# Attention and a cosine feed-forward: six plain blocks instead of four ahead of Strassen pairs

## The chip, the cores and the metric

The kernel runs on one core of a Trainium2 chip. Five engines work at once, each through its own instructions in a fixed order: TensorE (PE, matmuls; PEld is its weight loads), VectorE (DVE), ScalarE (ACT), GpSimd (POOL) and SyncE (SP, which here only issues transfers). Matmuls write to PSUM (eight banks of 128 x 512 floats), everything else lives in SBUF, inputs and outputs in HBM, and DMA queues move data between them. The metric is the device time of one execution in microseconds (us).

## The reference

Eight batches, eight heads, 576 positions, head size 64. Heads 0 to 3 see the last 32 positions ("local"), heads 4 to 7 see earlier positions of the same residue modulo 32 ("strided"). The result, 4608 tokens by 512, goes through a feed-forward with 2048 hidden columns and the activation h * cos(h).

```python
scores = scale * np.matmul(q, k.transpose(0, 1, 3, 2))
mask_local = (rel >= 0) & (rel < stride)
mask_strided = (rel >= 0) & (pos[None, :] % stride == pos[:, None] % stride)
...
attn = np.exp(scores)
attn = attn / (np.sum(attn, axis=-1, keepdims=True) + 1e-09)
return np.matmul(attn, v).astype(np.float32)
...
h = x @ w_in
g = h * np.cos(h)
return (g @ w_out).astype(np.float32)
```

## The kernel before

**Numbers in two halves.** Each matmul operand of the feed-forward is kept as a rounded part and a remainder (`hi`, `lo`), and a product is three matmuls: hi*hi, hi*lo, lo*hi. A split is one cast (ACT or DVE) and one subtraction (POOL, sometimes DVE).

**Blocks.** The 4608 tokens are 12 blocks of 384 (TB). A *plain* block goes through 16 chunks, one for each 128 hidden columns. A chunk (`chunk`, L475) is `hidden` (12 matmuls into one PSUM bank, L436), the curve h*cos(h) on ACT and DVE (L442 to L449), its split, and, three chunks later (LAG), `outer`: 9 matmuls into three accumulators (L460). A *pair* is two blocks multiplied by Strassen's recursion in Winograd's form: for each *quad* (a pair of hidden chunks, 8 quads in all) seven products of 6 matmuls (L684) into the banks a and b stand for the 48 matmuls of four chunks; DVE and ACT add the products (p1, u2, u3, h), `curved` makes g, and the outer matmuls (L712), 12 tiles of three a quad, are used one quad later as *fillings* between the products (FILL). The weights of the pairs, sums and differences of blocks of `w_in`, are formed once by `combine` (L519) from the weights in SBUF, written to HBM (wis, wos), and loaded again quad by quad (`load_quad`, L669).

**Attention** is cut into units: four strided and three local ones a batch, 56 in all. A unit is a load of q and k and one of v, score matmuls (L291 local, L343 strided), a softmax on DVE, POOL and ACT, a transposition (PE through L360, or DVE's L300), and product matmuls (L312, L374) whose result is copied to `x_t` or `x_l` and written to xT in HBM by ACT's queue. Outside the first stage a unit spreads over several chunks: in a burst (`burst`, L504) the products of unit k-3 and the scores of unit k are interleaved when they use PE in the same tile shape.

**Stages.** (1) The 14 units of batches 0 and 1. (2) Blocks 0 and 1 side by side, while the weights are loaded and split. (3) Blocks 2 and 3 with batches 2 to 4 beside them: bursts stand ahead of chunks as KNOTS says, and `combine` is called every third chunk. (4) Four pairs, with batches 5 to 7 beside the first 21 quads: scores in bank a, transposition in b, products in a and b, between the products of the quad. Stages 3 and 4 use different pools; stage 4 begins with `stage_x` (L646), which loads 4 x 2 pieces of x, forms 3 further operands each, and `split_operand` (L661) for all seven. At each later pair's boundary the seven operands are replaced one by one while the last quad uses them.

Chunks of stage 3 are counted from block 2 below, so chunk 0 is its first. Each engine runs its own list in order; a scheduler that models times writes the lists, and may put an instruction earlier than the code calls it. `in_turn` (L183) keeps PE's matmuls from block 2 on in the order of the code.

Of the kernel before, what the change touches and what calls it, by code (L numbers as in the profile page):

```python
# [26 lines left out]
P = 128  # L27
# [36 lines left out]
KNOTS = ((3, 0), (19, 16), (30, 23))  # L64
# [3 lines left out]
PLAIN = 4  # L68
NPAIR = (NTB - PLAIN) // 2
NQ = NFC // 2  # L70
PB = 5
FILL = (2, 2, 2, 2, 2, 1, 1)

# [7 lines left out]
def attention_cos_ffn(ctx, tc, qkl, vl, qkvs, w_in, w_out, eye, eye16, mask_l0, mask_l, mask_s, out):  # L81
# [5 lines left out]
    plain = ExitStack()  # L87
    ps_h = plain.enter_context(tc.tile_pool(name="ps_h", bufs=2, space=bass.MemoryType.PSUM, reuse_waits="tile"))
    ps_o = plain.enter_context(tc.tile_pool(name="ps_o", bufs=1, space=bass.MemoryType.PSUM, reuse_waits="tile"))
# [32 lines left out]
    wp = plain.enter_context(tc.tile_pool(name="wp", bufs=1, reuse_waits="tile"))  # L122
    wi_h, wi_l, wo_h, wo_l = [], [], [], []
    for f in range(NFC):
        for held, name, shape in (
            (wi_h, "wi_h", [P, NKC, P]), (wi_l, "wi_l", [P, NKC, P]), (wo_h, "wo_h", [P, DM]), (wo_l, "wo_l", [P, DM]),
        ):
            held.append(wp.tile(shape, F32R, name=f"{name}{f}"))
    xs = plain.enter_context(tc.tile_pool(name="xs", bufs=2 * NKC, reuse_waits="tile"))
# [61 lines left out]
    class Attention:  # L191
# [6 lines left out]
        def __init__(self, stack, plain, scores, transposed, products, ld_bufs):  # L198

            self.plain, self.banks = plain, None  # L200
# [12 lines left out]
        def bank(self, kind):  # L213
            pool, name = self.banks.pop(0) if self.banks else next(kind)
            return pool.tile([P, 512], F32, name=name)

        def score_bank(self, mask):
# [10 lines left out]
            if self.banks:  # L228
                return self.bank(None)
# [48 lines left out]
        def local(self, b, u):  # L278
# [49 lines left out]
        def strided(self, b, p, u):  # L328
# [10 lines left out]
            rows = GP if self.banks else GB  # L339
            s_ps = self.score_bank(mask)  # L340

            def score(t, i):
                self.scored = self.pe(nc.tensor.matmul(  # L343
                    s_ps[half(1 - i, rows), t * GB:(t + 1) * GB], qk[half(i), t * GB:t * GB + rows], k_t[half(i), t],
                    start=not self.plain, stop=True, skip_group_check=True,
                ))
# [3 lines left out]
                if rows == GP or SU * u + t // 2 * 2 + i < NG  # L350
# [80 lines left out]

    def hidden(j, f, x_hi, x_lo):
        h = ps_h.tile([P, 512], F32, name="h")[:, :TB]
# [22 lines left out]
    def outer(j, f, g_hi, g_lo, acc):  # L456
        for t in range(NTT):
# [7 lines left out]
            if f == NFC - 1:  # L465
                o = op.tile([P, DM], F32, name="o")
                if t % 2:
                    nc.vector.tensor_copy(out=o, in_=acc[t])
                else:
                    nc.scalar.copy(out=o, in_=acc[t])  # L470
                nc.sync.dma_start(out=out[j * TB + t * P:j * TB + (t + 1) * P, :], in_=o)
# [47 lines left out]
    def combine(sp, q):  # L519

        wf = sp.tile([P, 2, DM], F32, name="wf", bufs=1)
        for n, f in enumerate((q, q + NQ)):
            nc.gpsimd.tensor_tensor(
                out=wf[:, n], in0=wi_h[f].bitcast(F32).rearrange("p c n -> p (c n)"),
                in1=wi_l[f].bitcast(F32).rearrange("p c n -> p (c n)"), op=ALU.add,
            )
# [10 lines left out]

        s1 = formed(4, a21, a22, ALU.add)
        s2 = formed(0, s1, a11, ALU.subtract)
        formed(3, a11, a21, ALU.subtract)  # L540
        formed(6, a12, s2, ALU.subtract)
        for i, f, k in ((1, q, 0), (2, q, 1), (5, q + NQ, 1)):
            for part, w in enumerate((wi_h, wi_l)):
# [3 lines left out]
                )  # L547
        for f in (q, q + NQ):
            for part, w in enumerate((wo_h, wo_l)):
                nc.sync.dma_start(out=wos[f][:, part], in_=w[f].bitcast(F32))  # L550

    first = [x_operands() for _ in range(2)]
    with ExitStack() as loading:
        cv = loading.enter_context(tc.tile_pool(name="cv", bufs=3, reuse_waits="tile"))
        with ExitStack() as stack:
# [3 lines left out]
                stack, True, ((ps_h, "h"), (ps_h, "h"), (ps, "acc0")), ((ps_o, "acc0"), (ps_o, "acc1")),  # L559
# [21 lines left out]
        rp = plain.enter_context(tc.tile_pool(name="rp", bufs=2, side="right", reuse_waits="tile"))  # L581
        gp = plain.enter_context(tc.tile_pool(name="gp", bufs=LAG + 1, side="right", reuse_waits="tile"))
# [18 lines left out]
    with ExitStack() as stack:  # L601
        op = stack.enter_context(tc.tile_pool(name="op", bufs=3, reuse_waits="tile"))
        sp = stack.enter_context(tc.tile_pool(name="sp", bufs=1, reuse_waits="tile"))
        ps = stack.enter_context(tc.tile_pool(name="ps", bufs=1, space=bass.MemoryType.PSUM, reuse_waits="tile"))
        att = Attention(stack, False, *(((ps, f"acc{i}"),) for i in range(3)), ld_bufs=2)
# [25 lines left out]
    plain.close()  # L631

    with ExitStack() as stack:
        rp, gp = (
            stack.enter_context(tc.tile_pool(name=name, bufs=bufs, side="right", reuse_waits="tile"))
            for name, bufs in (("rp2", 3), ("gp2", 6))
# [269 lines left out]
```

## Time and profile before

| | |
|---|---|
| median of 3 runs | 1028.52 us (1023.87 to 1029.41) |
| the profiled execution | 1028.36 us, of which the span of instructions is 1026.6 |
| stages 1 and 2 with the first three chunks of block 2 | to 201.75 us |
| stage 3, the rest | to 387.95 us |
| stage 4 | to the end |

The busy share of an engine is an average over stages. A wait is put down to the instruction that ended last before it. The granted clock is the share of full speed that PE was given in a stretch (1.00 is 2.4 GHz, half of it 1.2 GHz). Ends of matmuls are modelled, so counts in a window can miss or add a few at its edges.

### The profile page before, as it was taken

How to read it: one execution, taken by the hardware profiler on the slowest of the kernel's cores; microseconds unless marked ns; L12 is line 12 of the kernel's file. 1: busy time of each engine (PE TensorE's matmuls, PEld its weight loads, DVE VectorE, ACT ScalarE, POOL GpSimd, SP SyncE). 2: the span in 40 equal slices, each digit the busy share in tenths (PEclk: the TensorE clock that was granted, in tenths of full speed). 3: DMA queues.
4: the chain of work that ended last, by engine and by line, in shares of the span. 5: the costliest groups of instructions: out<-in, count | busy, mean ns of one | idle time of the engine just before them, and what ended most of it. 6: DMA issues, size and time to landing. Idle time of an engine off the chain costs nothing. (4 is left out here: it accounts for less than half of the span.)

```text
span 1026.6 us, 20627 instructions
## 1 busy us (share of the span) xinstructions
PE 933.2 (91%) x7852; PEld 806.1 (79%) x7852; DVE 584.6 (57%) x1085; ACT 533.2 (52%) x1095; POOL 438.9 (43%) x434
## 2 busy tenths in 40 slices
PE   8779999998689992999987999989989989999998
PEld 5568999977578882887876887867878778898997
DVE  5667654487776525554567444546763545754453
ACT  3557776465466532554535444535654434654543
POOL 3645655589864325332345222325532223532221
PEclk9899999999899996899989899999999989999999
DMA  9768764346554228866555665655585546575501
GB/s 299 261 192 280 247 225 134 108 144 220 185 171 135 72 65 327 318 201 189 198 177 183 207 195 174 203 196 167 183 269 178 176 122 185 169 262 173 167 21 61
DMA packets 97618, 190.98 MB, mean 186 GB/s; under 512 B 10992, under 2 KB 35056, under 8 KB 97520
## 3 DMA queue, kind: packets, MB, share of 16 engines
q1 hardware_dynamic: 89024, 181.57, 53.8%
q10 hardware_dynamic: 8496, 8.09, 2.4%
q8 instruction: 62, 1.02, 0.4%
q14 instruction: 36, 0.29, 0.1%
HBM read 149.26 MB, written 40.37 MB: 185 GB/s over the span
## 5 line engine op out<-in xcount | busy, mean ns | idle before, releaser
L712 PE MATMUL acc<-wo,g_hi 128*128 128x512 f32 x768 | 246.8, 404 | 0.0
L699 POOL TENSOR_TENSOR g_lo<-r,g_hi 128x384 fp32r<-128x384 f32 x128 | 133.4, 1043 | 232.6 <-ACT g_hi L698 120.8
L684 PE MATMUL a<-xo_hi,wq 128*128 128x384 f32 x512 | 158.3, 350 | 8.4 <-DVE t_sb L245 7.0
L712 PEld LDWEIGHTS acc<-wo,g_hi 128*128 128x128 f32 x768 | 146.5, 194 | 15.1
L684 PE MATMUL b<-xo_hi,wq 128*128 128x384 f32 x384 | 124.0, 364 | 35.8 <-DVE x_l L324 23.5
L712 PE MATMUL acc<-wo,g_lo 128*128 128x512 f32 x384 | 153.2, 399 | 0.0
L693 DVE SCALAR_TENSOR_TENSOR r<-r,h 128x384 f32<-128x384 int32 x128 | 81.2, 634 | 76.2 <-ACT r L692 75.1
L453 POOL TENSOR_TENSOR g_lo<-r,g_hi 128x384 fp32r<-128x384 f32 x64 | 70.1, 1095 | 107.3 <-issue 56.2
L684 PEld LDWEIGHTS a<-xo_hi,wq 128*128 128x128 f32 x512 | 98.1, 195 | 16.6 <-DVE t_sb L245 8.3
L684 PEld LDWEIGHTS b<-xo_hi,wq 128*128 128x128 f32 x384 | 75.0, 198 | 41.6 <-DVE x_l L324 24.5
L694 ACT ACTIVATE r<-r,biases 128x384 f32<-128x384 f32 x128 | 78.9, 617 | 52.6 <-DVE r L693 51.9
L695 DVE TENSOR_TENSOR r<-r,h 128x384 f32<-128x384 f32 x128 | 85.7, 670 | 29.0 <-ACT r L694 27.5
L698 ACT CAST g_hi<-r 128x384 fp32r<-128x384 f32 x128 | 65.5, 512 | 66.6 <-DVE r L695 66.1
L436 PE MATMUL h<-x_hi,wi_h 128*128 128x384 f32 x256 | 89.1, 348 | 3.2 <-DVE r L449 3.1
L692 ACT ACTIVATE r<-h 128x384 int32<-128x384 f32 x128 | 67.0, 523 | 44.5 <-DVE h L788 21.9
L684 PE MATMUL a<-xo_lo,wq 128*128 128x384 f32 x256 | 88.5, 346 | 0.0
L712 PEld LDWEIGHTS acc<-wo,g_lo 128*128 128x128 f32 x384 | 74.6, 194 | 17.5
L436 PE MATMUL h<-x_hi,wi_l 128*128 128x384 f32 x256 | 86.3, 337 | 0.0
L436 PE MATMUL h<-x_lo,wi_h 128*128 128x384 f32 x256 | 85.9, 336 | 0.0
L460 PE MATMUL acc<-wo_h,g_hi 128*128 128x512 f32 x192 | 77.7, 405 | 0.0
L460 PE MATMUL acc<-wo_l,g_hi 128*128 128x512 f32 x192 | 77.0, 401 | 0.0
L460 PE MATMUL acc<-wo_h,g_lo 128*128 128x512 f32 x192 | 74.6, 396 | 0.0
(136 smaller groups left out, 1733.4 us busy)
## 6 DMA issues: line engine op xcount, KB each, us to landing
wq<-wis SPq DMA_DIRECT2D x224, 256.0 KB, 2.8
wo<-wos SPq DMA_DIRECT2D x64, 512.0 KB, 4.2
qk<-in_qkvs SPq DMA_DIRECT2D x32, 324.0 KB, 3.4
qk<-in_qkl SPq DMA_DIRECT2D x24, 416.0 KB, 3.7
out<-o SPq DMA_DIRECT2D x36, 256.0 KB, 2.6
raw<-in_w_in SPq DMA_DIRECT2D x16, 512.0 KB, 5.4
raw<-in_w_out SPq DMA_DIRECT2D x16, 512.0 KB, 3.7
wis<-sr SPq DMA_DIRECT2D x32, 256.0 KB, 2.2
```

The source lines that it names most:

```text
L436: mm = nc.tensor.matmul(h, w[f][:, c], x[c], start=(i == 0), stop=(i == len(ops) - 1))
L453: nc.gpsimd.tensor_tensor(out=g_lo, in0=r, in1=g_hi.bitcast(F32), op=ALU.subtract)
L460: mm = nc.tensor.matmul(acc[t], g[:, ts], w[f], start=(f == 0 and i == 0), stop=(f == NFC - 1 and i == 2))
L684: in_turn(nc.tensor.matmul(bank, w[:, n, c], part[:, c], start=start and i == 0, stop=stop and i == len(ops) - 1, skip_group_check=True,))
L692: nc.scalar.activation(out=k, in_=h, func=AF.Copy, scale=1.0 / (2.0 * math.pi), bias=0.25)
L693: nc.vector.scalar_tensor_tensor(out=r, in0=k, scalar=-2.0 * math.pi, in1=h, op0=ALU.mult, op1=ALU.add)
L694: nc.scalar.activation(out=r, in_=r, func=AF.Sin, bias=quarter)
L695: nc.vector.tensor_tensor(out=r, in0=r, in1=h, op=ALU.mult)
L698: nc.scalar.copy(out=g_hi, in_=r)
L699: nc.gpsimd.tensor_tensor(out=g_lo, in0=r, in1=g_hi.bitcast(F32), op=ALU.subtract)
L712: in_turn(nc.tensor.matmul(acc, g[gn][:, ts], w[:, wn], start=done == 0 and i == 0, stop=done == NFC - 1 and i == 2,))
```

## The change

Six blocks are plain and three pairs remain. All 42 units of batches 2 to 7 stand beside the 61 chunks of stage 3 (KNOTS), none in the pairs; both copies of `x_l` are ACT's. `combine` is cut in four parts, called one a chunk from chunk 14 on. From chunk 49 on `staging` loads and splits the operands of the first pair, into the x tiles of block 4 and weight slots that block 5 has used. All weights lie in one pool of 64 slots; in the pairs the slots 20 to 37 take the products' weights, 38 to 51 those of the outers, and 0 to 19 and 52 to 63 hold two sets of x operands, so that the next pair's operands are made while this pair runs. The last three outers of block 5 are the first fillings of the pairs.

```diff
-KNOTS = ((3, 0), (19, 16), (30, 23))
+KNOTS = ((3, 0), (13, 9), (59, 44))
...
-PLAIN = 4
+PLAIN = 6
...
+X_AT, WQ_AT, WO_AT, Y_AT = 0, 20, 38, 52
+SUMS_AT = 14
+STAGED_AT = 49
...
-            if self.plain:
-                nc.scalar.copy(out=x_t[1], in_=a_ps[1][:, :LQ])
-            else:
-                nc.vector.tensor_copy(out=x_t[1], in_=a_ps[1][:, :LQ])
+            nc.scalar.copy(out=x_t[1], in_=a_ps[1][:, :LQ])
...
+    def staging(pool, c, k, pieces):
+
+        at = (PLAIN + 2 * c) * TB
+        b12, b11, b22, b21, t1, t2, t4 = (
+            pool.tile([P, TB], F32, name=name) for name in ("b12", "b11", "b22", "b21", "t1", "t2", "t4")
+        )
+        for raw, row, n in ((b12, 0, 1), (b11, 0, 0), (b22, 1, 1), (b21, 1, 0)):
+            nc.sync.dma_start(out=raw, in_=xT[:, 2 * row + k, at + n * TB:at + (n + 1) * TB])
+        yield
+        nc.vector.tensor_tensor(out=t1, in0=b12, in1=b11, op=ALU.subtract)
+        nc.vector.tensor_tensor(out=t2, in0=b22, in1=t1, op=ALU.subtract)
+        for i, raw in enumerate((t2, b11, b21, b12, t1, t4, b22)):
+            if i == 2:
+                nc.vector.tensor_tensor(out=b12, in0=b22, in1=b12, op=ALU.subtract)
+                nc.vector.tensor_tensor(out=t4, in0=b21, in1=t2, op=ALU.subtract)
+            hi, lo = (piece() for piece in pieces[i])
+            nc.scalar.copy(out=hi, in_=raw)
+            nc.gpsimd.tensor_tensor(out=lo, in0=raw, in1=hi.bitcast(F32), op=ALU.subtract)
+            operands.setdefault((c, i), []).append((hi, lo))
+            if i % 2:
+                yield
+        yield
...
-        units = [unit for b in range(2, PB) for unit in att.units(b)]
+        units = [unit for b in range(2, B) for unit in att.units(b)]
...
+        sums = [part for q in range(NQ) for part in 4 * [combine(sp, q)]]
...
-            if n >= LAG + 1 and (n - LAG - 1) % 3 == 0 and (n - LAG - 1) // 3 < NQ:
-                combine(sp, (n - LAG - 1) // 3)
-        while pend:
-            outer(*pend.pop(0))
...
+            if n >= SUMS_AT and sums:
+                next(sums.pop(0))
+            if n == STAGED_AT:
...
+                staged = [part for k in range(2) for part in 5 * [staging(xg, 0, k, a_pieces[k])]]
+            if n > STAGED_AT and staged:
+                next(staged.pop(0))
...
+    y_pieces = in_xs + in_slots(range(Y_AT, Y_AT + 12)) + 4 * [
+        partial(yp.tile, [P, TB], F32R, name=name) for name in ("y_hi", "y_lo")
+    ]
+    pieces = a_pieces, (in_pairs(y_pieces[:14]), in_pairs(y_pieces[14:]))
...
+    wqs, wos_at = itertools.cycle(range(WQ_AT, WO_AT)), itertools.cycle(range(WO_AT, Y_AT))
+
+    def load_quad(q):
+        ws, os = [], []
+        for i in range(7):
+            w = slot(next(wqs))
+            nc.sync.dma_start(out=w.bitcast(F32), in_=wis[q][i].rearrange("p w n -> p (w n)"))
...
+    fillers = [partial(outer, *kept, tiles=(t,)) for kept in pend for t in range(NTT)]
...
+        if q == 0 and c + 1 < NPAIR:
+            staged = [part for k in range(2) for part in 5 * [staging(xg, c + 1, k, pieces[(c + 1) % 2][k])]]
+            next(staged.pop(0))
...
-            if n < len(units):
-                scores(units[n])
             use(3, b, False, False)
...
-            unit = units[n - 1] if 1 <= n <= len(units) else None
-            if unit:
-                turned(unit)
             use(6, a, False, True)
...
+        for _ in range(min(len(staged), 1 + (q % 3 == 1))):
+            next(staged.pop(0))
```

What the lists look like at three places. First PE, where the plain blocks end and the pairs begin, before (acc are the accumulators, a and b the pairs' banks):

```order
L460 MATMUL acc_3840<-wo_h_154,g_hi 128x512
L460 MATMUL acc_3840<-wo_l_155,g_hi 128x512
L460 MATMUL acc_3840<-wo_h_154,g_lo 128x512
L684 MATMUL b<-xo_hi_5182,wq 128x384
L684 MATMUL b<-xo_lo_5183,wq 128x384
L684 MATMUL b<-xo_hi_5182,wq 128x384 x2
L684 MATMUL b<-xo_lo_5183,wq 128x384
L684 MATMUL b<-xo_hi_5182,wq 128x384
L684 MATMUL a<-xo_hi_5188,wq 128x384
```

And now (s are weight slots, as weights and as x operands):

```order
L458 MATMUL acc_6494<-s_136,g_lo 128x512
L710 MATMUL b<-x_hi,s_7593 128x384
L710 MATMUL b<-x_lo,s_7593 128x384
L710 MATMUL b<-x_hi,s_7593 128x384
L710 MATMUL b<-s_7253,s_7593 128x384
L710 MATMUL b<-s_7254,s_7593 128x384
L710 MATMUL b<-s_7253,s_7593 128x384
L458 MATMUL acc_6492<-s_137,g_hi 128x512
L458 MATMUL acc_6492<-s_153,g_hi 128x512
L458 MATMUL acc_6492<-s_137,g_lo 128x512
```

Outer tiles of the last plain chunks now stand between the first products, where nothing stood.

Second DVE, in the first chunks with attention, before (sf are the weight sums, `x_hi` the cast of a loaded block of x):

```order
L300 STREAM_TRANSPOSE pt_l<-e_sb 128x384
L405 CAST x_hi<-x_lo 128x384
L324 COPY x_l<-acc_3299 128x192
L531 TENSOR_TENSOR sf<-wf 128x256
L245 TENSOR_TENSOR t_sb<-acc_2539,ms 128x324
L531 TENSOR_TENSOR sf<-sf,wf 128x256
L246 TENSOR_REDUCE mx<-t_sb 128x6
L405 CAST x_hi<-x_lo 128x384
```

And now DVE at the same place:

```order
L300 STREAM_TRANSPOSE pt_l<-e_sb 128x384
L264 TENSOR_SCALAR z<-z 128x6
L245 TENSOR_TENSOR t_sb<-acc_2539,ms 128x324
L534 TENSOR_TENSOR sf<-wf 128x256
L265 RECIPROCAL z<-z 128x6
L246 TENSOR_REDUCE mx<-t_sb 128x6
L534 TENSOR_TENSOR sf<-sf,wf 128x256
L401 CAST x_hi<-x_lo 128x384
```

The second copy of a local unit has left DVE (it follows the first one on ACT); the sums and the casts of loaded x have not moved.

Third, DVE and SP at the first quad, now. DVE (r of the last plain chunk, t and b of the second pair's staging, u the pairs' sums):

```order
L447 TENSOR_TENSOR r<-r,b 128x384
L619 TENSOR_TENSOR t_8302<-b_8298,b_8299 128x384
L774 TENSOR_TENSOR u_7691<-b,p_7690 128x384
L620 TENSOR_TENSOR t_8303<-b_8300,t_8302 128x384
L623 TENSOR_TENSOR b_8298<-b_8300,b_8298 128x384
```

and SP, which issues the loads of it (wis_162 are weights of the third quad, wos_171 of the fourth):

```order
L704 DMA s_7826<-wos_171 128x512
L704 DMA s_7825<-wos_171 128x512
L617 DMA b_8299<-xT 128x384
L617 DMA b_8301<-xT 128x384
L699 DMA s_7656<-wis_162 128x512
L617 DMA b_8298<-xT 128x384
```

Where DVE before had t, seven splits and then the first u, it now has one t of the next pair ahead of the first u, and that t's load stands on SP behind two slots that PE must free.

## Rows read from the trace of the kernel before

**Rows 1.** The page, busy time of PE (share of the span, instructions).
```profile
PE 933.2 (91%) x7852; PEld 806.1 (79%) x7852; DVE 584.6 (57%) x1085; ACT 533.2 (52%) x1095; POOL 438.9 (43%) x434
```
**Rows 2.** Windows: length, busy PE PEld DVE ACT POOL, granted clock, DMA share, GB/s.
```profile
201.70:299.60 97.90, 80.89 (x1123) 68.11 (x1122) 76.48 (x148) 57.90 (x136) 84.57 (x91) 0.93 0.54 183
299.60:387.95 88.35, 88.35 (x998) 77.14 (x990) 43.03 (x95) 44.20 (x94) 30.20 (x35) 1.00 0.30 93
387.95:413.00 25.05, 6.70 (x19) 5.45 (x18) 13.75 (x11) 7.25 (x16) 13.49 (x9) 0.56 1.01 372
413.00:840.00 427.00, 392.10 (x3055) 337.71 (x3055) 233.36 (x441) 212.03 (x429) 148.46 (x144) 0.95 0.61 197
840.00:1013.00 173.00, 170.05 (x888) 152.31 (x887) 90.49 (x150) 85.01 (x166) 54.55 (x50) 0.99 0.47 149
```
**Rows 3.** Waits of PE, 201.7 to 388 (us in total, times, longest).
```profile
PE acc L360 <- DVE x_l L324: 12.0, 3, 6.6
```
**Rows 4.** Timeline at the entry of the pairs (start, length, idle before).
```profile
394.91 0.96 DVE L655 TENSOR_TENSOR t<-b,b 128x768 f32<-128x768 f32 x1 [6.92 <-DMA b<-xT]
...
400.22 0.69 PE L684 MATMUL b<-xo_hi,wq 128*128 128x384 f32 x1 [12.27 <-ACT xo_hi L664]
```
**Rows 5.** Waits of PE, 413 to 1013.
```profile
PE b L684 <- DVE x_l L324: 23.5, 9, 3.6
```
**Rows 6.** Windows of L436 alone: length, PE busy (matmuls), clock, DMA share, GB/s.
```profile
153.72:195.37 41.65, 22.68 (x120) 1.00 0.35 117
201.75:299.60 97.85, 30.72 (x157) 0.93 0.54 183
299.61:348.82 49.21, 21.02 (x108) 1.00 0.39 122
```
**Rows 7.** Groups of ACT, 299.6 to 348.8: the softmax's first exponential.
```profile
L256 ACT ACTIVATE e_sb<-t_sb,biases 128x324 f32<-128x324 f32 (+1 forms) x7 | 4.1, 588 | 9.2 <-POOL t_sb L247 6.9 <-DMA xT<-x_l 2.3
```
**Rows 8.** Windows of L684 alone, in the pairs.
```profile
420.79:457.29 36.50, 17.47 (x85) 1.00 0.67 217
903.90:997.98 94.08, 51.08 (x252) 1.00 0.47 150
```
**Rows 9.** Chain that ended last, 810 to 830 (start, length, what).
```profile
811.09 1.39 PE acc L712 x6
812.49 1.06 PE a L684 x6
813.54 1.13 SPq L673
...
814.73 3.71 DMA b<-xT
...
818.53 0.96 DVE t L655
...
820.48 2.00 PE a L684 x6
822.49 2.26 PE acc L712 x6
```
**Rows 10.** DMA issues of the page (KB each, median us to landing).
```profile
wq<-wis SPq DMA_DIRECT2D x224, 256.0 KB, 2.8
```
**Rows 11.** Timelines of DVE and ACT, 260 to 272.
```profile
266.71 0.36 DVE L405 CAST x_hi<-x_lo 128x384 fp32r<-128x384 f32 x1 [3.63 <-DMA x_lo<-xT]
...
271.53 0.33 DVE L324 COPY x_l<-acc 128x192 f32<-128x192 f32 x1
...
270.33 0.31 ACT L320 COPY x_l<-acc 128x192 f32<-128x192 f32 x1
```
**Rows 12.** Groups of DVE, 201.7 to 299.6 (count, busy us, mean ns).
```profile
L258 DVE SCALAR_TENSOR_TENSOR e_sb<-t_sb,e_sb 128x324 f32<-128x324 f32 x8 | 8.1, 1013 | 1.5 <-ACT t_sb L257 1.5
...
L443 DVE SCALAR_TENSOR_TENSOR r<-r,h 128x384 f32<-128x384 int32 x14 | 7.5, 533 | 2.5 <-ACT r L442 2.5
```
**Rows 13.** The same group of DVE, 299.6 to 348.8.
```profile
L258 DVE SCALAR_TENSOR_TENSOR e_sb<-t_sb,e_sb 128x324 f32<-128x324 f32 x4 | 2.0, 496 | 4.1 <-ACT t_sb L257 4.1
```

More of the change, by code (lines that the diff above doesn't have):

```diff
@@ L120, in order, with slot @@
         )
[L122 to L129, printed above, removed]
+    wp = ctx.enter_context(tc.tile_pool(name="wp", bufs=1, reuse_waits="tile"))
+    def slot(n):
+        return wp.tile([P, DM], F32R, name=f"s{n}")
+    wi_h, wi_l, wo_h, wo_l = ([slot(4 * f + n) for f in range(NFC)] for n in range(4))
+    for held in (wi_h, wi_l):
+        held[:] = [t.rearrange("p (c n) -> p c n", c=NKC) for t in held]
+    xs = ctx.enter_context(tc.tile_pool(name="xs", bufs=2 * NKC, reuse_waits="tile"))
     xT = dram.tile([P, NKC, NTOK], F32, name="xT")
@@ L213, in bank @@
         def bank(self, kind):
-            pool, name = self.banks.pop(0) if self.banks else next(kind)
+            pool, name = next(kind)
             return pool.tile([P, 512], F32, name=name)
@@ L454, in hidden, with outer @@
         return g_hi, g_lo
-    def outer(j, f, g_hi, g_lo, acc):
-        for t in range(NTT):
+    def outer(j, f, g_hi, g_lo, acc, tiles=range(NTT)):
+        for t in tiles:
             ts = slice(t * P, (t + 1) * P)
@@ L465, in outer, with store @@
             if f == NFC - 1:
[L466 to L471, printed above, removed]
+                store(acc[t], t, j * TB + t * P)
+    def store(acc, t, at):
+        o = op.tile([P, DM], F32, name="o")
+        if t % 2:
+            nc.vector.tensor_copy(out=o, in_=acc)
+        else:
+            nc.scalar.copy(out=o, in_=acc)
+        nc.sync.dma_start(out=out[at:at + P, :], in_=o)
     pend = []
@@ L599, in attention_cos_ffn @@
                 chunk(2, f, cur, acc)
[L601 to L605, printed above, removed]
-        units = [unit for b in range(2, PB) for unit in att.units(b)]
+    op = ctx.enter_context(tc.tile_pool(name="op", bufs=3, reuse_waits="tile"))
@@ new lines, in attention_cos_ffn, with in_slots, in_pairs @@
+    operands = {}
+    def in_slots(numbers):
+        return [partial(lambda n: slot(n)[:, :TB], n) for n in numbers]
+    def in_pairs(pieces):
+        return [pieces[2 * i:2 * i + 2] for i in range(7)]
+    in_xs = 4 * [partial(xs.tile, [P, TB], F32R, name=name) for name in ("x_hi", "x_lo")]
+    with ExitStack() as attending:
+        ps = attending.enter_context(tc.tile_pool(name="ps", bufs=1, space=bass.MemoryType.PSUM, reuse_waits="tile"))
+        summing = ExitStack()
+        sp = summing.enter_context(tc.tile_pool(name="sp", bufs=1, reuse_waits="tile"))
+        att = Attention(attending, False, *(((ps, f"acc{i}"),) for i in range(3)), ld_bufs=2)
+        units = [unit for b in range(2, B) for unit in att.units(b)]
@@ new lines, in attention_cos_ffn, with outer_tile @@
+    accs = {}
+    fillers = [partial(outer, *kept, tiles=(t,)) for kept in pend for t in range(NTT)]
+    def outer_tile(c, t, g, w):
+        if (c, t) not in accs:
+            accs[c, t] = [(ps if t // NTT else ps_o).tile([P, DM], F32, name=f"acc{t % NTT}"), 0]
+        acc, done = accs[c, t]
+        accs[c, t][1] = done + 1
+        ts = slice((t % NTT) * P, (t % NTT + 1) * P)
+        for i, (gn, wn) in enumerate(((0, 0), (0, 1), (1, 0))):
+            in_turn(nc.tensor.matmul(
+                acc, g[gn][:, ts], w[wn], start=done == 0 and i == 0, stop=done == NFC - 1 and i == 2,
+            ))
+        if done == NFC - 1:
+            store(acc, t, (PLAIN + 2 * c) * TB + t * P)
@@ L813 @@
+    fill(len(fillers))
 _OUT = ((NTOK, DM), "float32")
```

281 lines of the change are left out of this document (108 added, 173 removed).

## The prediction

> **What bounds the kernel now.** I read the page first: the matmul engine (PE) is busy 933.2 of 1026.6 us, more than any other [rows 1]. So PE sets the time, and two questions remain: how long its work takes when nothing stops it, and where it is stopped. The windows by stage answer the second [rows 2]: PE is busy without a break in 299.60 to 387.95 and nearly so after 840, but loses 17.0 us in 201.70 to 299.60, 18.4 in 387.95 to 413.00 and 34.9 in 413 to 840; in the same three stretches the granted clock falls to 0.93, 0.56 and 0.95, so each wait is paid a second time in slow matmuls. The waits name the causes: in the first stretch mostly the bank that the copy `x_l` empties [rows 3], at the entry of the pairs the operands `xo_hi` [rows 4], in the pairs `x_l` again [rows 5].
>
> **Unit prices, from stretches without waits.** A plain chunk (12 matmuls into h, 9 into acc): 120 L436 matmuls, so 10 chunks, in 153.72 to 195.37, 4.165 us each. The 9 chunks of 299.61 to 348.82 (x108) took 49.21, so 11.7 more than nine clean ones [rows 6]; seven attention units pass there, one full cycle of their kinds (one exponential of L256 each [rows 7]): 1.68 us a unit beside plain work. A quad of a pair (42 products, 36 outer matmuls): 252 products, so 6 quads, in 903.90 to 997.98, 15.68 us each. The two quads of 420.79 to 457.29, with one unit each, took 36.50, so 2.57 us a unit beside pairs [rows 8].
>
> **The change, part by part.**
> (a) *One pair becomes two plain blocks.* 32 chunks come, 133.3 us, and 8 quads go, 125.4: plus 7.8 us.
> (b) *21 units move from the pairs into plain blocks*, where scores of one unit and products of another of the same kind are interleaved: 21 x (1.68 - 2.57) = -18.7 us.
> (c) *The waits in the pairs go.* A quad begins at 997.98, so the last product ends about 1013.7; from 387.95 that is 625.7 us. Clean: 32 quads x 15.68, less the last quad's twelve outer tiles, 8.3 (six outer matmuls 1.39 [rows 9]), is 493.4, and 21 units 54.0. So 78.3 us are lost: 18.4 idle at the entry, 37.8 in the pairs (34.9 and 2.9 [rows 2]), and some 22 in slow clock. With no attention there, only products, outers and their evacuation run in the pairs, as in 903.90 to 997.98, at clock 1.00.
> (d) *A new entry.* Before, loads of x began when the last plain outers were done; DVE stood 6.9 us for them, then came 28 splits, then the first product at 400.22 [rows 4]. Now x of the first pair is staged during blocks 4 and 5, and three outers are kept as filling. What can be late: bank b, freed by the chain of the last plain chunk, four steps of about 0.55 (as `r` of L443 [rows 12]) and their handovers, against 2.1 us of outers beside it: about 1.5 us. And u2: DVE's order has t_8302 of the second pair ahead of it, which needs b_8298, and SP issues that one behind s_7656, a slot that product 0 frees. The same chain stands in the trace of before, at an inner boundary: SP at wq, 3.71 us of a load into b, t, then PE's product late by the clock of 2.00 for 1.06 [rows 9]. Product 0 ends some 2.5 us after the last plain outer; with 1.1 in SP's line and 3.7 to land, as there, and 1.1 for two of DVE's instructions, u2 is there at 8.4. Product 3 wants it after two more products (2.1) and six outer tiles (4.2), at 8.8. It is hidden by 0.4 us; with a load of 6.9, as at the old entry, it costs 3. I take 5 us for the entry and 3 for the splits of the second and third pair, which pass mostly in quads 0 to 2 and 7 to 9: 8 lost in the pairs; bounds 2 (all hidden) and 25 (the entry as now: 387.95 to 413.00 held three products, 3.2 us, so 22 lost).
> (e) *The attention stage, now 61 chunks long.* Today's, 201.75 to 387.95, is 29 chunks (120.8), 21 units (35.3), three kept outers (6.3), and so 23.8 us lost: 17.0 idle [rows 2], the rest slow clock. POOL is busy 84.57 and DVE 76.48 of the first 97.90, because the weight sums run there: the order has them there in both kernels, whatever chunk the code calls them in. That stays, with four additions of 256 columns for two of 512. What goes is `x_l` on DVE, 12.0 us of the waits [rows 3]. The worst, 6.6 us, shows why I don't count all of it: DVE stood 3.63 us before a cast whose load was late, and the copy came at 271.53; but ACT's copy of the same unit came at 270.33, only 1.2 us before [rows 11]. ACT hangs on DVE's results, so I take half away, with half of the slow clock: 15 left. Then come some 20 chunks with units and no sums: no wait, as in 299.60 to 387.95. From chunk 34 on staging is new: three groups (two of the first pair, one of the second), each begun by a t on DVE that waits for a load of x, with the reductions `r` queued behind it, and PE behind their banks. A hold of 3.63 us cost 6.6 at worst; I take 3.3 and a little slow clock for each, 11 together. So 26 us are lost in this stage; bounds 10 (x_l's waits gone whole with their clock, loads early) and 60 (15 and the 45 of the second rival).
>
> A rule bears on this stage. In rows: `e_sb` (DVE, both operands in SBUF, 324 wide) took 1013 ns on average in the first stretch, where POOL was busy 86% [rows 2, 12], and 496 in 299.6 to 348.8, with no sums [rows 13], while `r`, with an operand in PSUM, took 533 in the first. That is the second rival's mechanism. The Trainium skill says the same in "GPSIMD Engine Reference", § 1. Specifications: POOL's SBUF interfaces are shared with VectorE, and DVE instructions with two SBUF inputs are among those that contend; the trace agrees. It speaks against the change, which puts splits on POOL and subtractions of two SBUF operands on DVE beside `e_sb`.
>
> **The sum**, from the profiled execution (span 1026.6, its own time 1028.36, so 1.8 outside; the median of the runs, 1028.52, is the same within 0.02%). Up to 201.75 PE's order is the same: 201.75. Then 61 chunks 254.1, 42 units 70.6, lost 26: 552.4. Three kept outers 6.3 and 24 quads 376.3: 935.0. Lost in the pairs 8, the end after the last tile 4.6 (1026.6 - 1013.7 - 8.3): 947.6, and 1.8: 949.4, **950 us** in round figures. The other way round, 1028.4 + 7.8 - 18.7 - 78.3 + 8 + 2 gives the same.
>
> **Rivals.**
> *1. Forecast:* 950; with (d) and (e) in their nearer bounds, 930 to 970.
> *2. The crowding comes back with the staging.* In 201.75 to 299.60 (13 chunks, x157, and 13 units) 97.85 us were 54.1 + 21.8 clean, so 1.68 lost a chunk [rows 6]. If staging crowds POOL and DVE so in the last 27 chunks with units, these lose 45 for my 11: 984. For: splits come to POOL, and DVE's two-operand instructions slow beside them. Against: sums cost POOL 48 operations in 13 chunks, the first pair's staging 14, in chunks 46 to 54.
> *3. The entry keeps its gap,* since the loads of weights for the pairs wait in SP's order behind slots that the last block frees: 22 for 5, 967. Against: SP's rows put both first quads' weights ahead of what waits.
> *4. Everything is hidden,* each loss at its lower bound: 950 - 16 - 6 = 928.
> *5. Slower: the pairs starve on their weights.* 18 slots for products, seven used by a quad, hold 2.6 quads where 20 did 2.9, and SP's loads stand in one line, each behind a slot that PE frees. If that line falls behind by one load in each quad, PE waits 2.8 us (landing of wq [rows 10]) and then runs slow, as at 820.48, where a product and six outers took 4.26 for 2.45 [rows 9]: 4.6 x 24 = 110 on the forecast, 1060. It decides from 3.3 us a quad. For: SP is in order. Against: some eighteen products lead, and the DMA share is 0.47 in 903.90 to 997.98 [rows 8].
> That the change does not do what it says, I exclude by the order: no attention matmul stands behind the first product.
>
> **Chances.** Forecast 0.69, second 0.15, third 0.07, fourth 0.06, fifth 0.03. Range 930 to 985: below it lies most of the fourth, above it half of the second and the fifth; the likeliest case's own is 930 to 970. What a measurement tells from no change is 0.5%, some 5 us: faster 0.96 (the first four, but for a second that grows much worse), same 0.01, slower 0.03.
>
> **What would show it.** Right: in the pairs 15.7 us a quad at clock 1.00, with no wait over 1 us from the third quad on; the entry under 5 us idle; plain chunks with a unit 5.8 us; PE's waits in the attention stage under 20 us, and most of them before 300. Wrong: waits of PE for `r` or for banks in the last 27 chunks with POOL over 80% busy (second); PE idle for 10 us near 550 behind SP (third); waits for weight slots in each quad (fifth).

## The result and the profile after

The changed kernel takes 963.11 us (median of four runs, 961.42 to 964.36) where the kernel before takes 1028.97 beside it; the ratio is 0.9365, with a 95% interval of 0.9325 to 0.9404. The profiled execution took 964.36 with a span of 962.5. The forecast was 950, so the change gave 66 us where I had written 79. PE's share of the span on the page, to set beside [rows 1]:

```profile
PE 911.6 (95%) x7876; PEld 797.0 (83%) x7876; DVE 542.3 (56%) x1022; ACT 520.4 (54%) x1084; POOL 436.4 (45%) x464
```

The windows of the changed kernel, to set beside [rows 2] (length, busy PE PEld DVE ACT POOL, granted clock, DMA share, GB/s). The first product now begins at 564.53; all before is plain blocks.

```profile
201.70:300.00 98.30, 84.52 (x1070) 72.35 (x1069) 74.28 (x143) 58.24 (x136) 86.51 (x107) 0.91 0.55 181
300.00:400.00 100.00, 95.05 (x1218) 82.61 (x1220) 56.81 (x121) 52.77 (x118) 43.57 (x50) 0.98 0.39 122
400.00:500.00 100.00, 96.11 (x1341) 83.41 (x1340) 58.98 (x129) 59.42 (x134) 45.18 (x51) 0.98 0.39 122
500.00:560.00 60.00, 58.65 (x602) 51.86 (x601) 28.04 (x59) 33.07 (x74) 27.97 (x30) 1.00 0.60 193
560.00:700.00 140.00, 134.80 (x664) 119.46 (x663) 74.07 (x119) 72.02 (x144) 59.06 (x56) 1.00 0.60 192
```

The pairs run at clock 1.00 with little idle time. The attention stage does not: its first 98 us are as bad as before (13.8 us idle at clock 0.91; before, 17.0 at 0.93), and the next 200 have some 9 us idle where 299.60 to 387.95 had none. The waits of PE, first in the attention stage (before: [rows 3]), then in the pairs (before: [rows 5]; engine, what, released by: us in total, times, longest):

```profile
PE acc L356 <- ACT x_l L321: 8.7, 5, 3.1
PE acc L370 <- ACT pt L360: 7.4, 7, 2.0
PE b L434 <- DVE r L447: 3.2, 1, 3.2
PE a L434 <- DVE r L447: 2.2, 1, 2.2
```

```profile
PE a L710 <- ACT p L773: 3.3, 3, 1.4
PE a L710 <- DVE h L787: 1.5, 1, 1.5
PE acc L739 <- ACT g_hi L724: 1.5, 1, 1.5
```

Five quads without a wait, by the products' line alone (before: [rows 8]): 78.47 / 5 = 15.69 us each, where 15.68 was forecast.

```profile
854.70:933.17 78.47, 42.59 (x210) 37.76 (x211) 1.00 0.44 138
```

The account by the forecast's own terms, in profiled executions. The attention stage ends 564.53 - 201.75 = 362.8 us after its start; clean it is 254.1 + 70.6, so 38.1 are lost, not 26. From the first product to the end of the last (948.32) are 383.8 us; clean, 24 x 15.68 + 6.3 - 8.3 = 374.3, so 9.5 are lost, not 8. From there to the end of the span are 14.2 us, not 12.9. The three differences come to 14.8 us; with them the forecast's sum of 949.4 is 964.2, where the profiled execution took 964.36.

Not all of the 38.1 us were lost in the stage. Its first burst stands at 201.75 in the kernel before and later here:

```profile
202.47 0.81 PE L339 MATMUL acc<-qk 64*54 64x54 f32 x24
```

So 0.7 us were lost ahead of it, and counted from its first burst the stage loses 37.4. The runs below differ more at this point, by up to 8 us, so they are compared from their own first burst.

The entry went as the forecast had it, step by step. DVE's timeline (start, length, idle before): the load of the second pair's x holds t for 5.88 us, u2 (L774) follows at 571.56 and ends at 572.11, and product 3 starts on time at 572.16.

```profile
563.92 0.55 DVE L447 TENSOR_TENSOR r<-r,b 128x384 f32<-128x384 f32 x1 [0.68 <-ACT r L444]
570.35 1.28 DVE L619 TENSOR_TENSOR t<-b,b 128x384 f32<-128x384 f32 x1 [5.88 <-DMA b<-xT]
571.56 0.55 DVE L774 TENSOR_TENSOR u<-b,p 128x384 f32<-128x384 f32 x1
572.03 0.54 DVE L620 TENSOR_TENSOR t<-b,t 128x384 f32<-128x384 f32 x1
```

What PE waits for at the entry is something else. Product 6 waits 1.51 us for the sum behind product 4 (`c22` in the code, L787), which DVE reaches only after a reduction, the copy of a finished output tile and a `t` of the second pair's next piece:

```profile
577.90 0.76 DVE L619 TENSOR_TENSOR t<-b,b 128x384 f32<-128x384 f32 x1
578.59 0.55 DVE L787 TENSOR_TENSOR h<-a,u 128x384 f32<-128x384 f32 x1
```

After it an outer tile waits 1.49 for g_hi and 0.52 for g_lo; with 0.42 before the first product PE idles 3.9 us in all.

One thing in the attention stage is new to me: loads that hold DVE, and through it everything, far from any sum. At 321.3 the casts of the next plain block's x (L401) get their turn on DVE, and the first waits 3.73 us. The exponential on ACT then waits 7.33, and `r` (L447), for which PE waits 2.19, comes at 331.98. DVE, then ACT, then PE:

```profile
325.03 0.36 DVE L401 CAST x_hi<-x_lo 128x384 fp32r<-128x384 f32 x1 [3.73 <-DMA x_lo<-xT]
...
331.98 0.55 DVE L447 TENSOR_TENSOR r<-r,a 128x384 f32<-128x384 f32 x1
```

```profile
330.28 0.56 ACT L256 ACTIVATE e_sb<-t_sb,biases 128x324 f32<-128x324 f32 x1 [7.33 <-POOL t_sb L247]
```

```profile
332.59 0.45 PE L434 MATMUL a<-x_hi,s 128*128 128x384 f32 x1 [2.19 <-DVE r L447]
```

That load is issued at 322.56, behind a unit's write of xT, about ten chunks ahead of where the code calls for it. At 417.41 a staging subtraction does the same (4.50 us behind a load of b).

### The profile page after: what moved, and what is told of

Its sections match the earlier page's. It is cut to its first block, busy times and chain, and to the rows that moved or that the text cites. A ratio compares the mean times of both kernels' runs of the same rounds, so it can differ in the third digit from the quotient of the medians.

```text
span 962.5 us, 20651 instructions
## 1 busy us (share of the span) xinstructions
PE 911.6 (95%) x7876; PEld 797.0 (83%) x7876; DVE 542.3 (56%) x1022; ACT 520.4 (54%) x1084; POOL 436.4 (45%) x464
## 5 line engine op out<-in xcount | busy, mean ns | idle before, releaser
L458 PE MATMUL acc<-s,g_hi 128*128 128x512 f32 x576 | 183.0, 402 | 0.0
L739 PE MATMUL acc<-s,g_hi 128*128 128x512 f32 x576 | 179.9, 394 | 1.5 <-ACT g_hi L724 1.5
L458 PEld LDWEIGHTS acc<-s,g_hi 128*128 128x128 f32 x576 | 107.4, 192 | 16.3
L739 PEld LDWEIGHTS acc<-s,g_hi 128*128 128x128 f32 x576 | 106.1, 188 | 12.7 <-ACT g_hi L724 1.9
L434 PE MATMUL a<-x_hi,s 128*128 128x384 f32 x384 | 110.7, 349 | 4.3 <-DVE r L447 4.2
L434 PE MATMUL b<-x_hi,s 128*128 128x384 f32 x384 | 110.2, 348 | 4.3 <-DVE r L447 4.3
L739 PE MATMUL acc<-s,g_lo 128*128 128x512 f32 x288 | 112.9, 392 | 0.5 <-POOL g_lo L725 0.5
L458 PE MATMUL acc<-s,g_lo 128*128 128x512 f32 x288 | 112.4, 395 | 0.0
L710 PE MATMUL a<-s,s 128*128 128x384 f32 x384 | 83.3, 338 | 1.5 <-DVE h L787 1.5
L434 PEld LDWEIGHTS a<-x_hi,s 128*128 128x128 f32 x384 | 71.8, 192 | 7.7 <-DVE r L447 5.2
L434 PEld LDWEIGHTS b<-x_hi,s 128*128 128x128 f32 x384 | 71.3, 190 | 7.9 <-DVE r L447 5.3
L710 PEld LDWEIGHTS a<-s,s 128*128 128x128 f32 x384 | 69.3, 188 | 5.9 <-DVE h L787 1.8
L434 PE MATMUL a<-x_lo,s 128*128 128x384 f32 x192 | 65.6, 341 | 0.0
```

The source lines that it names most:

```text
L434: mm = nc.tensor.matmul(h, w[f][:, c], x[c], start=(i == 0), stop=(i == len(ops) - 1))
L458: mm = nc.tensor.matmul(acc[t], g[:, ts], w[f], start=(f == 0 and i == 0), stop=(f == NFC - 1 and i == 2))
L710: in_turn(nc.tensor.matmul(bank, w[:, n, c], part, start=start and i == 0, stop=stop and i == len(ops) - 1, skip_group_check=True,))
L739: in_turn(nc.tensor.matmul(acc, g[gn][:, ts], w[wn], start=done == 0 and i == 0, stop=done == NFC - 1 and i == 2,))
```

## Experiments

Each run is given with its median, range and ratio to runs of the kernel before on the same chip.

**1. The copies x_l on DVE again.**

```
-            nc.scalar.copy(out=x_t[0], in_=a_ps[0][:, :LQ])
-            nc.scalar.copy(out=x_t[1], in_=a_ps[1][:, :LQ])
+            nc.vector.tensor_copy(out=x_t[0], in_=a_ps[0][:, :LQ])
+            nc.vector.tensor_copy(out=x_t[1], in_=a_ps[1][:, :LQ])
```

> The changed kernel with one part undone: the two copies x_l of each local unit are on DVE again, not on ACT. In the attention stage of the changed kernel (201.75 to 564) PE idles 24.0 us, and 8.7 of it still ends with a copy x_l, now ACT's; before, 12.0 of 17.0 ended with DVE's. First theory, the prediction's: half of the waits for x_l went with the engine, so they come back, some 6 us idle and 3 in slow clock: 963 + 9 = 972. Second theory: the copy is late because of what stands ahead of it in whichever queue it is in (on ACT casts that wait for a DMA of the sums, on DVE casts that wait for a load), so the engine hardly matters: 960 to 966, with other names for the same waits.

963.77 us (959.26 to 965.69), ratio 0.9381 (0.9352 to 0.9409): no difference. The edit reaches further than the change did: before, only the second copy was DVE's, and none in stage 1. The first burst of stage 3 stands at 205.56, 3.1 us later than in the changed kernel; from there the stage loses 38.1 us, as good as the 37.4 without the edit. PE's waits in it change their names:

```profile
PE acc L370 <- ACT pt L360: 15.3, 8, 3.6
PE acc L356 <- DVE z L265: 3.0, 2, 2.5
PE acc L356 <- DVE x_l L321: 2.0, 2, 1.3
```

The second theory holds in what it forecast. The prediction's term for x_l, half of 12.0 with half of the slow clock (some 9 us), is not there; at most a few us can hide in the noise.

**2. The weight sums left out.**

```
-        s1 = formed(4, a21, a22, ALU.add)
-        s2 = formed(0, s1, a11, ALU.subtract)
...
-        for i, f, k in ((1, q, 0), (2, q, 1), (5, q + NQ, 1)):
+        for i, f, k in ((4, q, 0), (0, q, 1), (3, q + NQ, 0), (6, q + NQ, 1)):
```

> The changed kernel with the arithmetic of the weight sums left out (the additions wf, the subtractions sf, the casts and remainders sr): the four summed pieces of each quad are written to HBM from plain weights by as many bytes of DMA. First theory: the sums beside attention crowd POOL (busy 86.5 of 98.3 us in 201.7 to 300) and through it DVE and ACT, and this is most of what the attention stage loses (24.0 idle and 13.7 in slow clock, 37.7 in all): 20 to 25 us go, 938 to 943, and the granted clock of that stretch rises from 0.91 to 0.98 or more. Second theory: the losses come from casts of x on DVE that wait for late loads and from the rhythm of the units, and the sums only stand beside them: 5 to 10 us go, 953 to 958.

947.17 us (941.35 to 951.87), ratio 0.9225 (0.9193 to 0.9257): 16 us less. In its profile (the fastest of the six) the first burst stands at 202.56 and the first product at 544.80, so 17.5 us are lost in the stage and not 37.4, and the first window runs at clock 1.00:

```profile
201.70:300.00 98.30, 95.32 (x1283) 82.35 (x1285) 59.65 (x133) 59.67 (x129) 44.95 (x52) 1.00 0.40 124
300.00:400.00 100.00, 91.57 (x1271) 79.80 (x1262) 56.88 (x126) 52.58 (x118) 42.09 (x48) 0.99 0.41 128
```

Between the two theories, nearer the first: the sums are half of what the stage loses. The other half stays, most of it in the window after, where there are no sums in either kernel.

**3. The sums spread over 32 chunks.** The additions wf on POOL and sf on DVE are ordered behind the latest remainder or reduction.

```
+                order(add, latest["pool"], "sums in turn")
...
+            order(nc.vector.tensor_tensor(out=t, in0=x, in1=y, op=op), latest["dve"], "sums in turn")
```

> The changed kernel with the same sums, each addition on POOL and DVE now ordered behind the remainder or reduction of the chunk whose code calls it, so that they stand over some 32 chunks instead of 17. First theory: the loss by crowding grows faster than the density, since units and sums together fill POOL to 87% in 201.7 to 300 and to 44% in 300 to 400; spread evenly it is about 60% in both: 10 us go, 953. Second theory: each sum costs PE the same wherever it stands (a cast that waits for its DMA holds ACT's queue): 960 to 966.

957.98 us (956.26 to 959.77), ratio 0.9330 (0.9303 to 0.9356): 5 us less, half of the first theory's 10. The intervals of the two ratios overlap, the ranges of the times don't, and in the profile the stage loses 32.6 us for 37.4, so I take it as a small gain. The windows:

```profile
201.70:300.00 98.30, 92.63 (x1240) 79.91 (x1239) 57.57 (x129) 56.88 (x124) 48.51 (x57) 0.98 0.39 120
300.00:400.00 100.00, 91.69 (x1210) 79.47 (x1208) 68.32 (x137) 56.97 (x135) 66.34 (x80) 0.97 0.49 162
400.00:500.00 100.00, 93.12 (x1193) 80.58 (x1193) 62.95 (x134) 57.30 (x135) 61.45 (x75) 0.97 0.48 153
```

PE idles 5.7 + 8.3 + 6.9 = 20.9 us here and 13.8 + 5.0 + 3.9 = 22.6 (before rounding) in the changed kernel. The waits moved with the sums, as the second theory has it. What was won is mostly clock: 0.97 at the lowest, not 0.91.

**4. The staging of the next pair called one quad later.**

```
-        if q == 0 and c + 1 < NPAIR:
+        if q == 1 and c + 1 < NPAIR:
```

> The changed kernel with the staging of the next pair begun one quad later (in quad 1 of a pair and not in quad 0). At the entry of the pairs u2 stands on DVE behind t of the second pair, which waits 5.88 us for its load of x (564.5 to 570.4), and PE idles 1.51, 1.49 and 0.52 us in 579 to 588. First theory, the prediction's: the load of the second pair's x behind slots of weights is what makes u2 and all that follows it late; with it out of the way the entry idles under 1 us and 3 to 4 us go: 959 to 960. Second theory: the gap comes from the long chain of the first quad (too few outers kept as filling), and the hold only moves one quad on: 962 to 964.

962.96 us (960.50 to 963.81), ratio 0.9375 (0.9348 to 0.9401): no difference. But the edit did not move the hold. The scheduler put `t` of the second pair on DVE where it had stood, ahead of u2:

```profile
572.07 1.28 DVE L619 TENSOR_TENSOR t<-b,b 128x384 f32<-128x384 f32 x1 [6.25 <-DMA b<-xT]
573.28 0.54 DVE L774 TENSOR_TENSOR u<-b,p 128x384 f32<-128x384 f32 x1
```

So the run decides between neither theory. That the hold itself delays no product is seen in the changed kernel's own trace, where product 3 starts as soon as u2 is there. The wait of product 6 for c22 stays, 1.5 us. Nine tiles of kept outers fill the places behind products 0 to 4, and none stands behind product 5; that a tile there would hide the wait was not tried.

**5 and 6. The 21 later units left out, where they stood before and where they stand now.**

```
-        units = [unit for b in range(PB, B) for unit in att.units(b)]
+        units = []
```

> The kernel before without the 21 attention units that stand in its pairs (those of the last three batches are left out; their rows of xT are filled from an input by twelve DMAs). First theory, the prediction's terms (b) and (c): the units cost their 21 x 2.57 = 54 us of clean work and nearly all that the pairs lose behind their entry, 37.8 us of waits and some 22 in slow clock: 1028 - 54 - 60 = 914. Second theory: the pairs lose by their own chains (operands built again at each new pair, loads of weights), so only the clean price goes: 974.

```
-        units = [unit for b in range(2, B) for unit in att.units(b)]
+        units = [unit for b in range(2, 5) for unit in att.units(b)]
```

> The changed kernel without the same 21 units (here they stand in plain chunks, the last of blocks 2 to 5; xT filled as in the run beside). First theory: they cost 21 x 1.68 = 35.3 us and the waits and slow clock that PE has in the attention stage from 360 on (5.2 idle, about 2 in slow clock): 963 - 43 = 920. Second theory: as dense as before, units beside plain chunks lose as much as units with sums, and much of the 37.7 lost goes with them: 905 or less. The difference of this run's gain and that of the run beside is what the place of the units is worth; the prediction has 18.7 + 60 for it.

The kernel before without them: 942.44 us (938.79 to 943.83), ratio 0.9157 (0.9131 to 0.9184), halfway between the theories. In its profile the last plain outer ends at 396.5 and the last product at 923.5; clean are 493.4, so its pairs lose 33.6 us. With the units they lost 77.8 (78.3 in the prediction, which had the end of the last product at 1013.7; the trace has 1013.1). So the units cost the pairs 54.0 us of clean work and some 44 of waits and slow clock, and 33.6 was the pairs' own. PE's waits there:

```profile
PE b L689 <- ACT xo_hi L669: 11.8, 1, 11.8
PE a L689 <- ACT p L777: 8.2, 8, 2.2
PE b L689 <- POOL xo_lo L671: 5.5, 1, 5.5
```

In both runs the twelve added DMAs are issued on ACT's queue between 53 and 65 us, in stages 1 and 2, and stage 3 begins later than without the edit: at 209.80 for 201.75, and here, for 202.47:

```profile
209.33 0.81 PE L339 MATMUL acc<-qk 64*54 64x54 f32 x24
```

These 8.1 and 6.9 us come ahead of the units that were left out and have nothing to do with them; that the DMAs cause them was not tested.

The changed kernel without them: 928.65 us (925.30 to 929.60), ratio 0.9013 (0.8987 to 0.9039), 34.5 less, and 41 less without the late beginning of stage 3. From its first burst to the first product at 529.42 its stage loses 30.7 us, where it loses 37.4 with them. So beside plain chunks these units cost their clean 35.3 us and 6.7 of waits and slow clock, 42.0 in all, close to the 43 of the first theory. In the pairs they cost 98: the place of the units is worth some 56 us, where the prediction had 18.7 + 60.

**7. No casts or subtractions ahead of their chunk.**

```
+        order(nc.vector.tensor_copy(out=out, in_=in_), latest["dve"], "no earlier than its chunk")
...
+            nc.vector.tensor_tensor(out=t1, in0=b12, in1=b11, op=ALU.subtract), latest["dve"],
```

> The changed kernel with the casts x_hi of load_x and the first two subtractions of each staging ordered on DVE behind the reduction of the chunk whose code calls them; they stood up to ten chunks ahead of it. Their loads wait for the units' writes of xT, and DVE with all that is queued behind waits for the loads (7.1 us in casts, 7.9 in subtractions t in 201.7 to 563). First theory: these holds are what is left of PE's waits once the sums are set aside (at 298, 332, 336 to 347, 411 to 423, some 9 us, and as much again in slow clock): 10 to 15 us go, 948 to 953. Second theory: the holds fall into slack of DVE, and the waits for the copies pt and x_l come from ACT's order: 960 to 965.

955.71 us (954.57 to 958.11), ratio 0.9285 (0.9260 to 0.9309): 7.4 less. The windows show the holds gone between 300 and 500, where 8.8 us of idle time become 1.7, while the first is as it was:

```profile
201.70:300.00 98.30, 85.04 (x1082) 72.99 (x1081) 77.86 (x144) 58.30 (x138) 87.65 (x107) 0.95 0.55 184
300.00:400.00 100.00, 99.69 (x1368) 87.11 (x1367) 60.81 (x134) 59.81 (x135) 46.07 (x54) 1.00 0.45 137
400.00:500.00 100.00, 98.62 (x1364) 85.99 (x1362) 59.72 (x129) 59.36 (x134) 49.50 (x56) 1.00 0.43 131
```

The order also delays block 2's own casts: the first burst stands at 204.50, 2.0 us later. From there to the first product at 552.92 the stage loses 23.7 us for 37.4, 13.7 less; the pairs lose 11.9, 2.4 more. The first theory has the cause and the size of the gain in the stage, of which some 4 us are paid back on either side of it. The run orders casts and staging subtractions together and does not tell which of them gave how much.

**8. Both orders.** The edits of runs 3 and 7 in one kernel.

```
+                order(add, latest["pool"], "sums in turn")
...
+        order(nc.vector.tensor_copy(out=out, in_=in_), latest["dve"], "no earlier than its chunk")
```

> The changed kernel with both orders, the sums over 32 chunks (957.98 alone, 5 less than the changed kernel) and the casts and subtractions not ahead of their chunk. First theory: two causes that add up, 958 less 10 to 15: 943 to 948. Second theory: both only shift work about on DVE and ACT, which are about as full as before: 955 to 960.

957.78 us (957.17 to 959.84), ratio 0.9305 (0.9282 to 0.9328): no better than either. PE idles 4.4, 5.8 and 6.1 us in the three windows. The two gains do not add. Why is not shown; the spread sums now stand where the holds were.

**9 and 10. More buffers for the sums; their casts on DVE.**

```
-            part = sp.tile([P, 2, 2 * P], F32R, name="sr", bufs=2)
-            nc.scalar.copy(out=part[:, 0], in_=t)
+            part = sp.tile([P, 2, 2 * P], F32R, name="sr", bufs=4)
+            nc.vector.tensor_copy(out=part[:, 0], in_=t)
```

The first of the two runs has only the buffers.

> The kernel of the run without early casts (955.7) with four buffers for the summed pieces sr in place of two. There ACT still waits 8.1 us in 201 to 420 for the DMA that writes an older sr away, with the copies x_l and pt that PE waits for behind it in ACT's order. First theory: sums cost PE through these holds of ACT; without them 5 to 8 us go, 948 to 951. Second theory: the sums cost PE by the time that they take on POOL and ACT, whatever they wait for: 953 to 957.

> As the run beside, and the casts of the sums (sr, 32 of about 0.4 us) are on DVE and not on ACT. If PE's waits for x_l and pt come from what the sums put into ACT's order, they shrink again: 944 to 949. If it is DVE and POOL that set the pace of the units beside the sums (DVE busy 78 and POOL 88 of 98 us in 201.7 to 300), nothing goes or some comes: 953 to 960.

With four buffers: 953.36 us (952.49 to 954.40), ratio 0.9275 (0.9247 to 0.9304), 2.3 below run 7, which the intervals don't tell apart. ACT's wait for the DMA is gone (7.6 us in 201.7 to 300 in run 7), but its casts now wait for DVE:

```profile
ACT sr L541 <- DVE sf L539: 14.6, 22, 2.0
```

With the casts on DVE as well: 963.10 us (962.42 to 965.00), ratio 0.9373 (0.9343 to 0.9403), ten worse. DVE is then busy 87.90 of 98.30 us, and PE idles 20.3:

```profile
201.70:300.00 98.30, 77.98 (x950) 66.81 (x949) 87.90 (x166) 44.90 (x97) 86.94 (x104) 0.93 0.52 176
```

Both times fit the second theories: beside the sums the pace is set by DVE and POOL, not by what ACT waits for. How much of it is POOL's own part, no run separates.

**11. The first pair staged at the entry.** The loads are ordered behind the last chunk's reduction, and the steps stand behind the loop.

```
+            if c == 0:
+                order(load, latest["dve"], "at the entry")
...
-            if n > STAGED_AT and staged:
-                next(staged.pop(0))
+        while staged:
+            next(staged.pop(0))
```

> The changed kernel with the x operands of the first pair not staged during blocks 4 and 5: their loads and subtractions are ordered behind the last plain chunk's reduction. First theory, the prediction's: staging ahead closes the entry's gap, which was 18.4 us idle and as much as 22 lost in the kernel before; it comes back, some 15 to 20 us, less 4 to 6 that staging costs the attention stage: 963 + 9 to 16 = 972 to 979. Second theory: the kept outers and product 0 to 2 hide most of it, and the gain in the pairs came from the units alone: 958 to 966.

981.27 us (980.63 to 984.03), ratio 0.9555 (0.9511 to 0.9599): 18 us more, just over the first theory's range. The entry's window and the products that wait:

```profile
550.00:580.00 30.00, 16.42 (x69) 13.33 (x68) 11.96 (x14) 12.18 (x24) 20.53 (x19) 0.76 0.46 144
```

```profile
564.68 0.44 PE L713 MATMUL b<-x_hi,s 128*128 128x384 f32 x1 [3.34 <-ACT x_hi L630]
567.53 0.69 PE L713 MATMUL b<-x_lo,s 128*128 128x384 f32 x1 [2.41 <-POOL x_lo L631]
575.48 0.69 PE L713 MATMUL b<-s,s 128*128 128x384 f32 x1 [6.94 <-ACT s L630]
```

The first product stands at 564.68, as late as with staging (564.53), but it has waited 3.34 us for its operand; the last plain outer is done earlier:

```profile
560.95 0.39 PE L460 MATMUL acc<-s,g_lo 128*128 128x512 f32 x1
```

From the first burst (203.51 here) to the end of this outer are 357.8 us, and 361.6 in the changed kernel (to 564.11). So staging the first pair ahead costs the attention stage 3.8 us, just under the 4 to 6 of the first theory. What it gives at the entry is the time from that outer to the end of the last product, 404.2 us here and 384.2 with staging: 20 us.

**12. Eight plain blocks and two pairs.**

```
-KNOTS = ((3, 0), (13, 9), (59, 44))
+KNOTS = ((3, 0), (13, 9), (91, 44))
-PLAIN = 6
+PLAIN = 8
-STAGED_AT = 49
+STAGED_AT = 81
```

> The changed kernel with eight plain blocks and two pairs, so that the same 42 units stand over 93 chunks and not over 61, the sums where they were. First theory: what the attention stage loses comes from the sums and from loads that hold DVE, not from how dense the units are; a pair given up costs 7.8 us and its staging 1 to 3 less: 968 to 971. Second theory: the loss is density, and thinner units lose a third less: 958 to 962.

951.91 us (951.59 to 954.03), ratio 0.9265 (0.9229 to 0.9301): 11 less than the changed kernel, where giving up a pair costs 7.8. From the first burst at 204.99 to the first product at 688.47 the stage loses 688.47 - 204.99 - 93 x 4.165 - 70.6 = 25.5 us (37.4 before this edit), and the pairs, 250.3 long against 248.9 clean, lose 1.4 (9.5). PE's waits in the stage:

```profile
PE acc L356 <- ACT x_l L321: 9.8, 4, 3.8
PE b L434 <- DVE r L447: 3.2, 1, 3.2
...
PE acc L370 <- ACT pt L360: 0.2, 1, 0.2
```

The waits for pt are gone (7.4 to 0.2), the others stay: the second theory, and more than it gave. Of the 8.1 us that the pairs lose less, 3.3 are idle time that the changed kernel has in quads 8 and 9 (693 to 718), where the third pair is staged, which is not there now; why the entry idles 1.2 us and not 3.9 is open. This is the lowest median of the versions that do all the work, not told apart from run 9 (953.36); with the order of run 7 it was not tried.

## Why the prediction was right, and where it was off

*(a) and (b), the trade of matmuls.* Quads at 15.69 us bear their price out. The unit's 1.68 fits a stretch far from the sums: 19 chunks, 4.165 us each, with 35 units on 46 chunks, so 14.5 units, make 103.4 us, and so long it is (by the line of the hidden products):

```profile
434.45:537.81 103.36, 44.43 (x228) 39.31 (x229) 1.00 0.45 141
```

Over the whole of their stretch 21 units cost 2.0 each with their waits (run 6). That a pair costs 7.8 more as plain blocks was not measured alone. By the traces of runs 5, 6 and 11 the parts add up: 56 for the place of the units and some 17 net for staging the first pair ahead, less 7.8, are 65 of the 66 us.

*(c), the waits in the pairs.* The sum was right, 78 down to 9.5. The reason was right for most of it: the units brought some 44 us of waits and slow clock. But 33.6 were there without them (run 5): about 18 idle at the entry with its slow clock, which staging ahead took (20 us in run 11), and some 12 behind it, mostly waits for `p`, which the prediction had put down to the attention. Why most of these 12 went too, no run shows.

*(d), the entry.* The steps of u2 came as forecast (t held by a load behind the weights, u2 just in time). The size, 3.9 us idle for the 5 I took, is right by chance: bank b cost 0.4 of its 1.5, u2 nothing of its 3, and the other 3.5 are c22 and g_hi with g_lo, which I did not have.

*(e), the attention stage.* This is where the forecast was off, 38.1 us for 26. By the windows some 21 of them lie before 300 (13.8 idle and, as an estimate, 0.09 of 84.5 in slow clock), where I had 15, and some 17 behind, where I had 11. "What goes is `x_l` on DVE", of which I took half, is refuted by run 1: a wait bears the name of the instruction that came last, and with ACT's copies it was as long. I had quoted the worst case myself, with ACT's copy only 1.2 us ahead of DVE's [rows 11]. "Then come some 20 chunks with units and no sums: no wait" failed by instructions that wait for loads ten chunks early: ordering the casts and the staging subtractions gave 7.4 us, most of it between 300 and 500 (run 7). Of the 11 us set against staging, the first pair's two groups cost 3.8 (run 11). The sums cost 16 to 20 us (run 2), more than the 15 that I had left for all of their stretch.

*Rivals.* The second did not come: from 430 to 560 PE idles 1.35 us, with POOL busy 36.5 of 60 in 470 to 530. The crowding that it speaks of fits the stretch with the sums (runs 2 and 10). The third did not come either, with 3.9 us idle at the entry and none of it for weights; run 11 shows what an entry without staging costs. The fifth left no sign: no product waits for a weight. The signs I had named fit but two: PE's waits in the attention stage were 24.4 us and not under 20, and two waits over 1 us stand behind the third quad (1.01 and 1.44, for p).

## What to carry to other kernels

A wait is named after the instruction that came last; before counting on moving that instruction to another engine, look at when its partner there was ready, since it may be late for the same reason. An instruction that waits for a load is put at its own place in an in-order queue, not as early as its data might be there: here DVE's casts and subtractions, ten chunks early, held units, chunks and PE. Side work beside matmuls can be cheaper where it is thin: with 42 units over 93 chunks the stage lost 12 us less than over 61, where the extra plain work cost 7.8; that it is the thinness alone, run 12 does not separate. An order given in the code need not arrive in an engine's list: run 4 changed a call and left the instruction where it was, so read the list before reading the time. And a run that leaves work out is compared from a mark that both share: run 6 began its stage 6.9 us later, which would have passed for free units.

## What the runs showed of the hardware

DVE's instructions with two operands in SBUF are slowed by POOL more than (d) had reckoned, which gave t and u2 together 1.1 us; they took 1.76 (570.35 to 572.11). In the fence on the entry above, t (L619) takes 1.28 us and the same form (L620) 0.54; at 570.22 POOL begins a subtraction of 1.01 us:

```profile
570.22 1.01 POOL L627 TENSOR_TENSOR s<-t,s 128x384 fp32r<-128x384 f32 x1
573.66 1.02 POOL L627 TENSOR_TENSOR y_lo<-b,y_hi 128x384 fp32r<-128x384 f32 x1 [2.44 <-ACT y_hi L626]
```

DVE's third subtraction, 572.49 to 573.04, stands between POOL's two and takes 0.55.

The Trainium skill gives the reason in "GPSIMD Engine Reference", § 1. Specifications: POOL's SBUF interfaces are shared with VectorE. The traces agree, with a factor of 1.28 / 0.54 = 2.4 for one instruction.

DVE's casts from SBUF to SBUF, with one operand, vary as much in run 10. The 32 casts of 128x256 take 268 to 1105 ns (mean 555; ACT's take 400 in the changed kernel). One that begins where POOL passes from one instruction to the next (273.15) takes 0.28; one that begins within POOL's 282.05 to 283.24 takes 0.98 and ends 0.15 us after it:

```profile
273.13 0.28 DVE L541 CAST sr<-sf 128x256 fp32r<-128x256 f32 x1
282.41 0.98 DVE L541 CAST sr<-sf 128x256 fp32r<-128x256 f32 x1
282.05 1.19 POOL L456 TENSOR_TENSOR g_lo<-r,g_hi 128x384 fp32r<-128x384 f32 x1
```
